# The end of a gated SSM/attention mix: one q half multiplied straight out of PSUM, the projection redistributed, the last tile added from PSUM and stored in halves

## The chip, the core and the metric

One core of one Trainium2 chip runs the whole kernel. The metric is the device time of one execution in microseconds (us); before the change it is 224.88 us, the median of three runs (224.69, 224.88 and 225.51). The profiled execution is another one, and its span, from its first to its last instruction, is 222.5 us.

The engines are named as in the profile: PE is TensorE (matmuls), PEld its weight loads, DVE is VectorE, ACT is ScalarE, POOL is GpSimd, SP is SyncE, which here only issues DMAs. "SPq" and "ACTq" are the sequencers of SP and ACT while they issue a DMA.

## The reference

The inputs are bf16 tensors of 2048 positions by 640 columns. Two branches read the same q, and a gate mixes them:

```
x = A_q;  g = sigmoid((x * gate_w).sum(-1, keepdims=True))
a = A_q * (long_convolution(shift(A_k) * A_v, A_ssm_k) + (shift(A_k) * A_v) * A_ssm_D)   # FFT of length 4096
b = local_attention(B_x @ wqkv; 32 heads of 20, window 8, dilation 2) @ wo
out = g * a + (1 - g) * b
```

The end of the kernel therefore needs three things for each output tile: `y`, the result of the last stage of the inverse transform; `g * q`, which is made earlier; and `(1 - g) * b`, the scaled output of the projection by `wo`. The output is `y * (g * q) + (1 - g) * b`.

## The kernel before, in words

The kernel is recorded by many small generators ("streams"): each yields a request for an engine, and a string (ORDER, L115 to L124) names, letter by letter, the stream whose request is granted next. So the order on every engine is written out by hand. The letter `s` grants a step of `outproj`, `t` a step of `final`, `u` and `v` a step of `load_q` for the first and the second half of q; a `-` takes the second engine that a request allows. Every engine works through its own list in order, and a wait of one instruction holds up all that stand behind it on that engine.

PSUM is cut into four slots of two banks (`plan = Steps(4)`). A matmul group takes a slot, or half of one, and the evacuation that reads the result gives it back.

The change lies in what happens after the last stage but one of the inverse transform (`inverse1`, L826 to L841, matmuls at L835, evacuated to `UC` by the helper at L243 on ACT and L245 on DVE). From there on four things are left:

- `final` (L893 to L930). The 16 output tiles of 128 positions are done in six groups of 3, 3, 2, 3, 3 and 2 tiles (`TAIL`). A group takes two PSUM slots: PE runs 32 small matmuls a tile (L912), and the result `y` lies in the first slot for columns 0 to 319 and in the second for columns 320 to 639. Both are copied to `yb`, one by ACT (L243) and one by DVE (L245), except the third group, where ACT copies both. Then DVE multiplies `yb` into the q tile in place (L924), adds the projection `bl` (L926), and SP stores the group with four DMAs (L929), one for each 32 partitions. In the last group ACT issues two of the four.
- `outproj` (L859 to L878). Each tile of the projection is done in two halves of 320 columns. A half is five matmuls (L869) into half a PSUM slot; ACT (L874), once DVE (L876), scales it by `omg`, which is 1 - g, and writes it to `bl`. Of the 32 halves 11 are done earlier in the kernel, 21 between and behind the groups of `final`: 4, 3, 4, 4, 4 and 2.
- `load_q` (L880 to L891). DVE multiplies the 16 tiles of q by g (L890). Eight of these stand between the steps of the first three groups.
- The end of the program (L965): SP waits for the landing of every DMA, and the engines meet at a barrier.

The DMAs that SP and ACT issue report their landing on eight semaphores (DMAHW0 to DMAHW7 in the instruction lists), which are given out in turn in the program's order. A DMA waits until the DMA that had its semaphore before it has landed.

Of the kernel before, what the change touches and what calls it, by code (L numbers as in the profile page):

```python
# [18 lines left out]
D = 640  # L19
# [29 lines left out]
KROWS = [(42, 64), (20, 42), (0, 20)]  # L49
TAIL = [(0, 3), (3, 3), (6, 2), (8, 3), (11, 3), (14, 2)]  # L50
# [65 lines left out]
a-aa-aw-wa-aw-ww-wiiai-iiaaiaa-aia-iii-aiaa-ii-iiii-ii-iiiicifffccccw-wwww-wwwwfwwwwf-wffffwwwwwwcwcccccwwwdw-wdwddddi-wfccccccii  # L116
-iiidfifddiiiieiifiiffiieidddiiiiiicddiwdxwexxxxxxxxxxccccffcfffffffffeccc-xcfcccccccccccccccccccccccccccccccccccccccccccidi-iiddd
ii-iddifd-iifxdddxedidffdfddefcicccii-iddiedd-icddlie-iiiyf-yddccdixiyyfy-xe-ydddexixdxddyyfyy-xcccxcccxffcccccccccccccciiiiciiccd
ciieddffdcccffdd-iiieiifiidididxdiffffffexididxdfeidid-i-xfxxyyy-yyexyey-xyyfyxccccccccciccccc-xcccc-idddidx-i-xxddddi-x-ijdddfjff
ejiddcciddcceiiiidddiiiiiffgg-ideieddd-ii-igigddiddeddjddeyjjyyyeeyyy-yyyy-yyyycc-yyyy-ycccccyyccccccccccccccclccccdddddz-zzd-zddd  # L120
z-zzzz-zzccczz-zzzzzz-zeddddedcdzdd-zedddoezdddd-zzo-zz-zjuddedddzedzz-zzzeezzz-zzooozz-z101-0010-1u111-111111-1o101-00o00-000000o
-00001011-1r-rr-r000u0r-r10111r00o00oooo2222-r0r-r000000000oqssss11110sssssss0s01111ssss2ss21111ssss222222222oooooooo222222244111p
313333p31333333333333413333uu4uuu444444444444444u54vv55u-5555-55-55-55-5555555tuut-ttssssssvvtvvstttstssssssv-tttvtttstssvv-ssvtvs
ttstst-ttssssssstttst-ttsssssssstttts-tssstt  # L124
# [91 lines left out]
def kernel(  # L216
# [642 lines left out]
    def outproj():  # L859
# [4 lines left out]
        for t in range(16):  # L864
            for n in range(2):
                g = yield Req("P", 0.0, [ev(f"oT{ft}") for ft in range(NDT)], take=1, half=1, pe=(5, 137.0, 272.0, 133.0))
                op = psum(g)[:, 0:320]
                for ft in range(NDT):
                    nc.tensor.matmul(op, lhsT=oT[:, ft].rearrange("p h m a -> p a (h m)")[:, t, :], rhs=wo[:, ft, 320 * n:320 * n + 320],  # L869
                                     start=(ft == 0), stop=(ft == NDT - 1), skip_group_check=True)  # L870
                r = yield Req("AD", dict(A=370.0, D=400.0), [g.done], give=g.banks)
# [5 lines left out]
            mark(f"bl{t}", r)  # L877
# [15 lines left out]
    def final():  # L893
        yield Req("N", 0.0, [ev("i10")])
        yb2 = p0.tile([128, 2, 3, D], BF, name="yb2", tag="H0")
        ybfree = [Ev(-1), Ev(-1)]
        for n, (t0, m) in enumerate(TAIL):
# [18 lines left out]
            es = []  # L916
            for k in range(2):
                r = yield Req("AD", n=320 * m, deps=[g.done, ybfree[n % 2]], give=[g.banks[k]])
# [51 lines left out]
```

## Time and profile before

| what | value |
|---|---|
| device time, median of 3 runs | 224.88 us |
| span of the profiled execution | 222.5 us |
| median less that span | 2.4 us |
| busy in the span: PE, DVE, ACT | 204.3, 185.0, 174.9 us |
| the last inverse-transform matmul (L835) to the first matmul of `final` | 1.1 us in which PE is idle |
| matmuls of `final` and the projection, 196.2 to 216.6 us | 20.4 us, PE busy for all of it |
| from the last matmul to the end of the span | 5.9 us |

The page's own time is the span; what lies around it, 2.4 us to the median, is the launch and the difference between the executions, and no view shows it in pieces. Times in the rows are us from the start of the span. In a timeline row the first number is the start, the second the time from the start of the first instruction of the row to the end of its last, "xN" the number of instructions merged in it, and a bracket at the end tells how long the engine was idle before and which work ended that. Instructions on one engine overlap by some tens of nanoseconds, so the start of the next row is the better measure of a step. In a row of groups the two numbers behind the bar are the busy time of all and the mean of one in ns.

### The profile page before, as it was taken

The numbers are of one execution on the slowest core, as the hardware profiler recorded it, in microseconds if no ns is written. First come the engines' busy times: TensorE is split into PE (matmuls) and PEld (weight loads), VectorE is DVE, ScalarE is ACT, GpSimd is POOL, SyncE is SP. The second block draws the span as 40 slices with busy tenths as digits, with TensorE's granted clock in tenths as the row PEclk, the third lists the DMA queues.
The fourth block names the chain that finished last, engine by engine and source line by source line (L and its number), as shares of the span: only waits on it lengthen the run. The fifth ranks groups of instructions, "written<-read, shape, count | busy, mean of one in ns | idle before, by whom it ended". The sixth has DMA issues, their size and how long they took to land.

```text
span 222.5 us, 8401 instructions
## 1 busy us (share of the span) xinstructions
PE 204.3 (92%) x3577; PEld 165.8 (75%) x3577; DVE 185.0 (83%) x261; ACT 174.9 (79%) x253; POOL 51.1 (23%) x129
## 2 busy tenths in 40 slices
PE   7999999999999999699997867999999999979990
PEld 3777987696777577466685756889888899979880
DVE  4745778997998898569898978998999997859992
ACT  0264487769998898599999988998999999478770
POOL 7980711470617044402450000000000000000000
PEclk9999999999999999999999699999999999999999
DMA  6999789599999999803993396678567082003645
GB/s 199 349 237 275 188 180 205 133 168 149 208 182 197 163 151 155 140 4 52 183 171 74 85 214 152 172 174 213 122 142 227 4 184 55 3 3 91 152 106 136
DMA packets 69049, 33.35 MB, mean 150 GB/s; under 512 B 51476, under 2 KB 66708, under 8 KB 69012
## 3 DMA queue, kind: packets, MB, share of 16 engines
q1 hardware_dynamic: 65684, 27.66, 61.3%
q0 software_dynamic: 2880, 4.90, 9.9%
q8 instruction: 28, 0.46, 1.0%
q10 hardware_dynamic: 448, 0.26, 0.4%
q14 instruction: 9, 0.07, 0.1%
HBM read 19.51 MB, written 2.62 MB: 100 GB/s over the span
## 4 chain that ended last, share of the span: by engine, by line
PE 51%; DVE 20%; ACT 10%; DMA 8%; issue 7%; POOL 2%; DVEq 0%; POOLq 0%; ACTq 0%
PE PS L568 14%; PE PS L521 8%; ACT ETall L650 6%; PE PS L835 6%; DMA kb<-stg 6%; DVE UC L245 5%; PE PS L869 4%; PE PS L724 4%; PE PS L674 3%; DVE SX L245 3%; PE PS L642 3%; DVE q L926 2%; DVE yb L245 2%; ACT H L243 2%; DVE q L924 2%
## 5 line engine op out<-in xcount | busy, mean ns | idle before, releaser
L650 ACT ACTIVATE ETall<-PS 121x912 bf16<-121x912 f32 (+1 forms) x80 | 63.8, 864 | 8.1 <-PE PS L642 7.7
L568 PE MATMUL PS<-xT,Wqk 128*128 128x342 bf16 (+1 forms) x300 | 49.7, 310 | 0.6 <-ACT stg L243 0.3
L243 ACT CAST UC<-PS 128x1024 bf16<-128x1024 f32 (+2 forms) x49 | 44.4, 1030 | 4.0 <-DVE UC L245 3.1
L568 PEld LDWEIGHTS <-Wqk 128*128 128x128 bf16 x300 | 27.4, 97 | 14.3 <-issue 0.5
L521 PE MATMUL PS<-WvT,xT 128*121 128x320 bf16 x180 | 27.5, 300 | 0.1
L467 DVE TENSOR_TENSOR KX<-KX 128x1280 bf16<-128x1280 bf16 x32 | 25.3, 820 | 0.3
L618 POOL DMA_DIRECT2D qb<-stg x29 | 14.6, 506 | 45.8 <-ACT stg L243 30.5
L869 PE MATMUL PS<-wo,oT 128*128 128x320 bf16 x160 | 24.4, 302 | 0.1
L521 PEld LDWEIGHTS <-xT 128*121 128x121 bf16 x180 | 23.4, 134 | 1.4
L243 ACT CAST stg<-PS 128x363 bf16<-128x363 f32 (+1 forms) x39 | 17.1, 471 | 7.8 <-PE PS L568 7.5
L869 PEld LDWEIGHTS <-oT 128*128 128x128 bf16 x160 | 21.1, 145 | 1.5 <-issue 0.5
L724 PEld LDWEIGHTS <-G 64*128 64x128 bf16 x512 | 18.2, 93 | 4.9 <-issue 3.7
L618 POOL DMA_DIRECT2D kb<-stg x36 | 18.1, 511 | 15.8 <-ACT stg L243 7.6
L642 PE MATMUL PS<-qb,kb 31*128 31x114 bf16 x576 | 16.0, 212 | 5.1 <-DMA kb<-stg 2.3
L245 DVE CAST stg<-PS 128x342 bf16<-128x342 f32 (+1 forms) x21 | 11.0, 522 | 11.7 <-PE PS L568 9.4
L642 PEld LDWEIGHTS <-kb 31*128 31x128 bf16 x576 | 9.4, 93 | 13.5 <-issue 9.8
L674 PEld LDWEIGHTS <-ETall 121*128 121x128 bf16 x576 | 17.4, 96 | 2.1 <-issue 0.5
L674 PE MATMUL PS<-VW,ETall 121*128 121x63 bf16 (+2 forms) x576 | 18.2, 184 | 0.6 <-DVE SX L245 0.3
L835 PE MATMUL PS<-F,Hw 128*128 128x128 bf16 x160 | 18.1, 219 | 0.0
L874 ACT ACTIVATE bl<-PS,omg 128x320 bf16<-128x320 f32 x31 | 16.1, 566 | 2.4 <-PE PS L869 1.9
L835 PEld LDWEIGHTS <-Hw 128*128 128x128 bf16 x160 | 17.9, 114 | 0.0
L245 DVE CAST UC<-PS 128x1024 bf16<-128x1024 f32 x13 | 15.3, 1219 | 2.6 <-ACT UC L243 1.2
(75 smaller groups left out, 334.1 us busy)
## 6 DMA issues: line engine op xcount, KB each, us to landing
xn<-in_A_q_dram SPq DMA_DIRECT2D x8, 320.0 KB
h_lin<-in_A_ssm_k_dram SPq DMA_DIRECT2D x16, 160.0 KB
vin<-in_A_v_dram SPq DMA_DIRECT2D x8, 320.0 KB
Hw<-H SPq DMA_DIRECT2D x8, 320.0 KB
q<-in_A_q_dram SPq DMA_DIRECT2D x8, 320.0 KB
Hw<-SX SPq DMA_DIRECT2D x8, 320.0 KB
kb<-stg POOLq DMA_DIRECT2D x28, 85.1 KB, 5.5
out_dram<-q SPq DMA_DIRECT2D x16, 120.0 KB
```

Of the source, the lines that this page charges most:

```text
L243: nc.scalar.copy(dst, src)
L245: nc.vector.tensor_copy(dst, src)
L467: eng.tensor_tensor(d, kin[:, n + 3 - j:n + 3 - j + m, :], w.to_broadcast([128, m, QC]), ALU.mult)
L521: nc.tensor.matmul(ps[0:BK, 0:320], lhsT=xT[:, dt, s0:s0 + BK], rhs=Wv[:, dt, 320 * hp:320 * hp + 320], start=(dt == 0), stop=(dt == NDT - 1))
L568: nc.tensor.matmul(ps[:, 0:n], lhsT=Wqk[:, dt, w, 128 * ft:128 * ft + 128], rhs=xT[:, dt, s0:s0 + n], start=(dt == 0), stop=(dt == NDT - 1))
L618: (nc.sync if near else nc.gpsimd).dma_start(dst[r0:r0 + rows, 0:wd], stg[fa - f0:fb - f0, 0:wd])
L642: nc.tensor.matmul(psum(g, h4 // 2)[:, h4 % 2, BQ * bb:BQ * bb + BQ], lhsT=kb[r:r + DH + NF, BK * b:BK * b + 128], rhs=qb[r:r + DH + NF, B ...
L650: nc.scalar.activation(ETall[0:BK, e, :, 0:BQ * nb], psum(g, k)[0:BK, :, 0:BQ * nb], ACT.Exp, scale=SCALE)
L674: nc.tensor.matmul(O[:, (b - b0) // 6, c0:c0 + 21 * nh], lhsT=ETall[0:BK, e, hh, BQ * bb:BQ * bb + 128], rhs=VW[0:BK, b, 4 * t + h4:4 * t ...
L724: nc.tensor.matmul(ps[:, c, 160 * jj:160 * jj + 160], lhsT=G[rows, j0 + jj, 64 - 64 * rr:192 - 64 * rr], rhs=Am[rows, rr].rearrange("p o ( ...
L835: nc.tensor.matmul(d, lhsT=st[(key, P)][:, c, o + il // 4, :, il % 4], rhs=M[:, k, :], start=(k == 0), stop=(k == 1), skip_group_check=True)
L869: nc.tensor.matmul(op, lhsT=oT[:, ft].rearrange("p h m a -> p a (h m)")[:, t, :], rhs=wo[:, ft, 320 * n:320 * n + 320], start=(ft == 0), s ...
```

## The change

`final` copies only the first half of the columns to `yb` (ACT, always). The second half is multiplied by q directly out of PSUM by DVE, and then the first half by a second, shorter multiply. The addition of `bl` and its store stay, but for the last tile (15) they fall away: there `outproj` waits until q * y of the tile is there (event `z15`), and one DVE instruction scales the projection half in PSUM by `omg` and adds the tile to it. Each half of that tile is then stored by two DMAs, one from SP and one from ACT, 64 partitions each. The two DMAs that ACT issued for the last group go to SP, and cover tile 14 alone.

The order changes too. The projection halves stand 2 ahead of the first group and 4, 3, 3, 3, 2 and 4 behind the six groups, and all eight multiplies of the second half of q stand ahead of the first group. Up to the last matmul of `inverse1` the order is the same as before.

```diff
+LATE = 15
...
             for n in range(2):
...
+                if t >= LATE:
+                    yield Req("D", 400.0, [g.done, ev(f"z{t}")], give=g.banks)
+                    reg = st["q1"][:, t % 8, 320 * n:320 * n + 320]
+                    nc.vector.scalar_tensor_tensor(reg, op, omg[:, t:t + 1], reg, ALU.mult, ALU.add)
+                    for gh in range(2):
+                        (nc.scalar if gh else nc.sync).dma_start(raw(outf, (32 * gh + 2 * t) * D + 320 * n, [[D, 2], [64 * D, 32], [1, 320]]), reg[64 * gh:64 * gh + 64])
+                    continue
...
-        yb2 = p0.tile([128, 2, 3, D], BF, name="yb2", tag="H0")
+        yb2 = p0.tile([128, 2, 3, 320], BF, name="yb2", tag="H0")
...
-            es = []
-            for k in range(2):
-                r = yield Req("AD", n=320 * m, deps=[g.done, ybfree[n % 2]], give=[g.banks[k]])
-                copy(r.eng, yb[:, 0:m, 320 * k:320 * k + 320].rearrange("p t (q c) -> p q t c", q=2),
-                     pss[k][:, :, 0:160 * m].rearrange("p q (t c) -> p q t c", c=160))
-                es.append(r.done)
-            yield Req("D", 68.0 + 0.52 * 640 * m, es + [ev(f"qg{t0 // 8}"), ev("qi1")])
             reg = st[f"q{t0 // 8}"][:, t0 % 8:t0 % 8 + m, :]
-            nc.vector.tensor_tensor(reg, yb[:, 0:m, :], reg, ALU.mult)
+            zs = [reg[:, :, 320 * k:320 * k + 320] for k in range(2)]
+            zq = [z.rearrange("p t (q c) -> p q t c", q=2) for z in zs]
+            y = [pss[k][:, :, 0:160 * m].rearrange("p q (t c) -> p q t c", c=160) for k in range(2)]
+            r0 = yield Req("A", n=320 * m, deps=[g.done, ybfree[n % 2]], give=[g.banks[0]])
+            nc.scalar.copy(yb[:, 0:m].rearrange("p t (q c) -> p q t c", q=2), y[0])
+            yield Req("D", 75.0 + 1.04 * 320 * m, [g.done, ev(f"qg{t0 // 8}"), ev("qi1")], give=[g.banks[1]])
+            nc.vector.tensor_tensor(zq[1], y[1], zq[1], ALU.mult)
+            r = yield Req("D", 68.0 + 0.52 * 320 * m, [r0.done])
+            nc.vector.tensor_tensor(zs[0], yb[:, 0:m], zs[0], ALU.mult)
...
+            m = min(m, LATE - t0)
+            reg = reg[:, 0:m]
...
             for gg in range(4):
-                (nc.scalar if n == len(TAIL) - 1 and gg > 1 else nc.sync).dma_start(raw(outf, (32 * (gg // 2) + gg % 2 + 2 * t0) * D, [[64 * D, 32], [2 * D, m], [1, D]]),
+                nc.sync.dma_start(raw(outf, (32 * (gg // 2) + gg % 2 + 2 * t0) * D, [[64 * D, 32], [2 * D, m], [1, D]]),
                                   reg[32 * gg:32 * gg + 32])
```

Three places show what moved. The first is ACT from its last evacuations of `inverse1` (`UC`) on; before, this is its list (`yb` is the copy of y, `bl` a projection half, `q_3452` the second half of q):

```order
L243 CAST UC<-PS 128x128x8 x14
L243 CAST yb_3616<-PS 128x2x3x160
L874 ACTIVATE bl<-PS,omg 128x320 x4
L243 CAST yb_3616<-PS 128x2x3x160
L874 ACTIVATE bl<-PS,omg 128x320 x3
L243 CAST yb_3616<-PS 128x2x2x160 x2
L874 ACTIVATE bl<-PS,omg 128x320 x3
L243 CAST yb_3616<-PS 128x2x3x160
L874 ACTIVATE bl<-PS,omg 128x320 x4
L243 CAST yb_3616<-PS 128x2x3x160
L874 ACTIVATE bl<-PS,omg 128x320 x4
L243 CAST yb_3616<-PS 128x2x2x160
```

And this is ACT's list at the same place with the change:

```order
L244 CAST UC<-PS 128x128x8 x14
L882 ACTIVATE bl<-PS,omg 128x320 x2
L930 CAST yb_3616<-PS 128x2x3x160
L882 ACTIVATE bl<-PS,omg 128x320 x4
L930 CAST yb_3616<-PS 128x2x3x160
L882 ACTIVATE bl<-PS,omg 128x320 x3
L930 CAST yb_3616<-PS 128x2x2x160
L882 ACTIVATE bl<-PS,omg 128x320 x3
L930 CAST yb_3616<-PS 128x2x3x160
L882 ACTIVATE bl<-PS,omg 128x320 x3
L930 CAST yb_3616<-PS 128x2x3x160
L882 ACTIVATE bl<-PS,omg 128x320 x2
```

Two projection halves now stand ahead of the first copy, and the fifth group has two behind it instead of four; the matmuls stand in the same order on PE.

The second place is DVE in the last two groups. Before:

```order
L245 CAST yb_3616<-PS 128x2x3x160
L924 TENSOR_TENSOR q_3452<-yb_3616,q_3452 128x1920
L926 TENSOR_TENSOR q_3452<-q_3452,bl 128x1920
L245 CAST yb_3616<-PS 128x2x2x160
L924 TENSOR_TENSOR q_3452<-yb_3616,q_3452 128x1280
L926 TENSOR_TENSOR q_3452<-q_3452,bl 128x1280
```

With the change:

```order
L932 TENSOR_TENSOR q_3452<-PS,q_3452 128x2x3x160
L934 TENSOR_TENSOR q_3452<-yb_3616,q_3452 128x3x320
L941 TENSOR_TENSOR q_3452<-q_3452,bl 128x1920
L932 TENSOR_TENSOR q_3452<-PS,q_3452 128x2x2x160
L934 TENSOR_TENSOR q_3452<-yb_3616,q_3452 128x2x320
L941 TENSOR_TENSOR q_3452<-q_3452,bl 128x640
L875 SCALAR_TENSOR_TENSOR q_3452<-PS,omg,q_3452 128x320 x2
```

The copy from PSUM has become the multiply, the other multiply is half as wide, and two instructions for tile 15 end the list.

The third place is SP's list of stores from the fifth group on, with the semaphores that each waits for. Before:

```order
L929 DMA out_dram<-q_3452 32x3x640 [waits DMAHW5_49,DVE_49]
L929 DMA out_dram<-q_3452 32x3x640 [waits DMAHW6_49]
L929 DMA out_dram<-q_3452 32x3x640 [waits DMAHW7_49]
L929 DMA out_dram<-q_3452 32x3x640 [waits DMAHW1_49]
L929 DMA out_dram<-q_3452 32x2x640 [waits DMAHW3_49,DVE_49]
L929 DMA out_dram<-q_3452 32x2x640 [waits DMAHW4_49]
```

With the change:

```order
L943 DMA out_dram<-q_3452 32x3x640 [waits DMAHW5_49,DVE_49]
L943 DMA out_dram<-q_3452 32x3x640 [waits DMAHW6_49]
L943 DMA out_dram<-q_3452 32x3x640 [waits DMAHW7_49]
L943 DMA out_dram<-q_3452 32x3x640 [waits DMAHW2_49]
L943 DMA out_dram<-q_3452 32x640 [waits DMAHW3_49,DVE_49]
L943 DMA out_dram<-q_3452 32x640 [waits DMAHW4_49]
L943 DMA out_dram<-q_3452 32x640 [waits DMAHW5_49]
L943 DMA out_dram<-q_3452 32x640 [waits DMAHW6_49]
L877 DMA out_dram<-q_3452 2x32x320 [waits DMAHW7_49,DVE_49]
L877 DMA out_dram<-q_3452 2x32x320 [waits DMAHW0_49,DVE_49]
```

SP issues six stores after the fifth group instead of two. The one that had DMAHW0 before SP's last store is ACT's first store of tile 15, and those that had DMAHW5, 6 and 7 are stores of the fifth group. ACT's two stores, of tile 15, each wait for DVE and for stores of the third and fourth group.

More of the change, by code (lines that the diff above doesn't have):

```diff
@@ L115 @@
 ORDER = """
[L116 to L124, printed above, removed]
+a-aa-aw-wa-aw-ww-wiiai-iiaaiaa-aia-iii-aiaa-ii-iiii-ii-iiiicifffccccw-wwww-wwwwfwwwwf-wffffwwwwwwcwcccccwwwdw-wdwddddi-wfcccccci
+i-iiidfifddiiiieiifiiffiieidddiiiiiicddiwdxwexxxxxxxxxxccccffcfffffffffeccc-xcfcccccccccccccccccccccccccccccccccccccccccccidi-ii
+dddii-iddifd-iifxdddxedidffdfddefcicccii-iddiedd-icddlie-iiiyf-yddccdixiyyfy-xe-ydddexixdxddyyfyy-xcccxcccxffcccccccccccccciiiic
+iiccdciieddffdcccffdd-iiieiifiidididxdiffffffexididxdfeidid-i-xfxxyyy-yyexyey-xyyfyxccccccccciccccc-xcccc-idddidx-i-xxddddi-x-ij
+dddfjffejiddcciddcceiiiidddiiiiiffgg-ideieddd-ii-igigddiddeddjddeyjjyyyeeyyy-yyyy-yyyycc-yyyy-ycccccyyccccccccccccccclccccdddddz
+-zzd-zdddz-zzzz-zzccczz-zzzzzz-zeddddedcdzdd-zedddoezdddd-zzo-zz-zjuddedddzedzz-zzzeezzz-zzooozz-z101-0010-1u111-111111-1o101-00
+o00-000000o-00001011-1r-rr-r000u0r-r10111r00o00oooo2222-r0r-r000000000oqssss11110sssssss0s01111ssss2ss21111ssss222222222oooooooo
+222222244111p313333p31333333333333413333uu4uuu444444444444444u54vv55u-5555-55-55-55-5555555ssssuuvvvvvvvvvvttttttsssssssstttttts
+sssssttttttssssssttttttsssssstttttssssttttttsssstssss
 """
@@ L876, in outproj @@
                     nc.vector.tensor_scalar(dst, op, omg[:, t:t + 1], None, ALU.mult)
-            mark(f"bl{t}", r)
+            if t < LATE:
+                mark(f"bl{t}", r)
         mark("outproj", g)
@@ L915, in final @@
             yb = yb2[:, n % 2]
-            es = []
-            for k in range(2):
-                r = yield Req("AD", n=320 * m, deps=[g.done, ybfree[n % 2]], give=[g.banks[k]])
-                copy(r.eng, yb[:, 0:m, 320 * k:320 * k + 320].rearrange("p t (q c) -> p q t c", q=2),
-                     pss[k][:, :, 0:160 * m].rearrange("p q (t c) -> p q t c", c=160))
-                es.append(r.done)
-            yield Req("D", 68.0 + 0.52 * 640 * m, es + [ev(f"qg{t0 // 8}"), ev("qi1")])
-            reg = st[f"q{t0 // 8}"][:, t0 % 8:t0 % 8 + m, :]
-            nc.vector.tensor_tensor(reg, yb[:, 0:m, :], reg, ALU.mult)
+            reg = st[f"q{t0 // 8}"][:, t0 % 8:t0 % 8 + m, :]
+            zs = [reg[:, :, 320 * k:320 * k + 320] for k in range(2)]
[7 more added lines that the diff above has]
+            nc.vector.tensor_tensor(zs[0], yb[:, 0:m], zs[0], ALU.mult)
+            ybfree[n % 2] = r.done
+            for t in range(t0, t0 + m):
+                mark(f"z{t}", r)
+            m = min(m, LATE - t0)
+            reg = reg[:, 0:m]
             r = yield Req("D", 100.0 + 0.52 * 640 * m, [ev(f"bl{t}") for t in range(t0, t0 + m)])
             nc.vector.tensor_tensor(reg, reg, st["bl"][:, t0:t0 + m, :], ALU.add)
-            ybfree[n % 2] = r.done
             for gg in range(4):
-                (nc.scalar if n == len(TAIL) - 1 and gg > 1 else nc.sync).dma_start(raw(outf, (32 * (gg // 2) + gg % 2 + 2 * t0) * D, [[64 * D, 32], [2 * D, m], [1, D]]),
+                nc.sync.dma_start(raw(outf, (32 * (gg // 2) + gg % 2 + 2 * t0) * D, [[64 * D, 32], [2 * D, m], [1, D]]),
                                   reg[32 * gg:32 * gg + 32])
```

## The prediction, written before the changed kernel was run

> **What bounds the kernel now.** I read the page first, then the busy time by stretches of the end, the chain of waits, and the timelines of PE, ACT, DVE and SP.
>
> ```profile
> span 222.5 us, 8401 instructions
> ```
>
> The busy time by stretches (columns: stretch, length, busy time and instruction count of each engine, granted clock, share of the DMA engines, GB/s):
>
> ```profile
> 195.10:196.20 1.10, 0.00 (x0) 0.00 (x0) 0.00 (x0) 1.07 (x2) 0.00 (x0) 1.00 0.00 0
> 196.20:216.60 20.40, 20.38 (x617) 18.26 (x616) 18.64 (x25) 15.35 (x26) 0.00 (x0) 1.00 0.37 93
> 216.60:218.30 1.70, 0.06 (x1) 0.00 (x0) 1.58 (x2) 0.53 (x1) 0.00 (x0) 1.00 0.69 169
> 218.30:220.40 2.10, 0.00 (x0) 0.00 (x0) 0.00 (x0) 0.00 (x0) 0.00 (x0) 1.00 0.92 248
> 220.40:222.50 2.10, 0.00 (x0) 0.00 (x0) 0.00 (x0) 0.00 (x0) 0.00 (x0) 0.85 0.01 4
> ```
>
> Four parts, then: 1.1 us in which PE is idle while ACT ends its evacuations; 20.4 us of PE without a gap; 1.7 us of ACT and DVE behind the last matmul; and 4.2 us without any compute, in the first half of which the stores drain. The chain of waits goes through DVE in the long part:
>
> ```profile
> 195.14 1.04 ACT UC L243
> 196.22 1.06 PE PS L912 x96
> ...
> 215.69 0.74 DVE yb L245
> ...
> 216.53 0.84 DVE q L924
> ...
> 217.46 0.83 DVE q L926
> ```
>
> PE and DVE are both nearly full there (20.38 and 18.64 of 20.40), so a saving on one alone would be held by the other. The change touches both, and the end of the stores as well, so I follow all three.
>
> **PE.** Its timeline:
>
> ```profile
> 196.22 1.02 PE L912 MATMUL PS<-UC,SX 32*32 32x160 bf16 x96 [1.14 <-ACT UC L243]
> 197.17 2.94 PE L869 MATMUL PS<-wo,oT 128*128 128x320 bf16 x20
> 200.04 1.03 PE L912 MATMUL PS<-UC,SX 32*32 32x160 bf16 x96
> 200.99 2.26 PE L869 MATMUL PS<-wo,oT 128*128 128x320 bf16 x15
> 203.18 0.76 PE L912 MATMUL PS<-UC,SX 32*32 32x160 bf16 x64
> 203.87 2.94 PE L869 MATMUL PS<-wo,oT 128*128 128x320 bf16 x20
> ...
> 215.08 1.58 PE L869 MATMUL PS<-wo,oT 128*128 128x320 bf16 x10
> ```
>
> By the starts, a group of three tiles takes 0.95 us (196.22 to 197.17), one of two 0.69, four projection halves 2.87 (197.17 to 200.04), three 2.19, so a further half 0.68 and two halves 1.51. Before, PE ends at 215.08 + 1.51 = 216.59.
>
> No matmul is added or removed; two halves move into the gap from 195.08 (196.22 - 1.14) on. They need only PSUM and the projection's inputs, and the slots that they take are those whose reading ends with this row of DVE and with the first of these three on ACT, both by 194.5:
>
> ```profile
> 189.82 4.62 DVE L245 CAST UC<-PS 128x1024 bf16<-128x1024 f32 x4 [0.58 <-PE PS L835]
> 193.32 2.84 ACT L243 CAST UC<-PS 128x1024 bf16<-128x1024 f32 x3 [3.07 <-DVE UC L245]
> ```
>
> They take till 196.59, 0.37 us past the old start of the first group, which itself waits for ACT's last evacuation (till 196.16). The same work then follows in the order 3 tiles, 4 halves, 3, 3 halves, 2, 3 halves, 3, 3 halves, 3, 2 halves, 2, 4 halves: 195.08 + 1.51 + 4 x 0.95 + 2 x 0.69 + 2 x 2.87 + 3 x 2.19 + 1.51 = 215.59. **PE ends 1.0 us earlier.** If the gap were not filled, this term would be nothing.
>
> **DVE.** The prices, from the groups of instructions:
>
> ```profile
> L686 DVE TENSOR_TENSOR VW<-PS,rd 114x960 bf16<-114x960 f32 x8 | 9.3, 1158 | 0.3
> L686 DVE TENSOR_TENSOR VW<-PS,rd 114x480 bf16<-114x480 f32 x8 | 5.3, 658 | 0.4
> L756 DVE TENSOR_TENSOR SX<-UC,SX 128x960 bf16<-128x960 bf16 x10 | 6.5, 651 | 0.0
> L756 DVE TENSOR_TENSOR SX<-UC,SX 128x640 bf16<-128x640 bf16 x1 | 0.5, 489 | 0.0
> L245 DVE CAST yb<-PS 128x960 bf16<-128x960 f32 x4 | 4.6, 1153 | 2.2 <-PE PS L912 2.2
> L245 DVE CAST yb<-PS 128x640 bf16<-128x640 f32 x1 | 0.8, 818 | 0.0
> L924 DVE TENSOR_TENSOR q<-yb,q 128x1920 bf16<-128x1920 bf16 x4 | 4.6, 1159 | 0.4
> L876 DVE TENSOR_SCALAR bl<-PS,omg 128x320 bf16<-128x320 f32 x1 | 0.5, 546 | 0.0
> ```
>
> The kernel already has a two-input DVE instruction that reads PSUM (L686), at 1158 ns for 960 elements: the multiply costs what the copy did (1153). The other multiply shrinks from 1159 to 651. So a group of three saves 0.5 us of DVE. The eight multiplies by g (one takes 0.38 us, two 0.67, so 0.30 for each further one) leave the stretch for the idle time ahead of it, where they run from 195.0 to 197.5 behind the two that end there now, done as the first group's matmuls are (196.59 + 0.95 = 197.54).
>
> ```profile
> 194.35 0.67 DVE L890 TENSOR_SCALAR q<-q,g_nat 128x640 bf16<-128x640 bf16 x2
> 201.26 0.38 DVE L890 TENSOR_SCALAR q<-q,g_nat 128x640 bf16<-128x640 bf16 x1
> ```
>
> Together that is about 5 us less in the stretch (8 x 0.30 and 6 x 0.5 at most). DVE stops being the bound and waits for PE; this saving is worth nothing by itself. It is only the cover for the first term: with DVE as full as before, PE's 1.0 us would have been lost to it.
>
> The exact point is the fifth group. Its second half behind it is done on PE at 195.08 + 16.95 = 212.03 (the sum above up to there). ACT needs 0.64 from there, as from 216.59 to the end of the last row here:
>
> ```profile
> 216.70 0.53 ACT L874 ACTIVATE bl<-PS,omg 128x320 bf16<-128x320 f32 x1 [0.15 <-PE PS L869]
> ```
>
> so DVE adds the group from 212.7 to 213.9 (1.16, as L926 before), where before it ended at 215.69. Behind that stand on DVE: the multiply of the last group out of PSUM 0.82 (price of the 640-element copy), the other 0.49, the addition of tile 14 0.49, and two scale-and-add instructions for tile 15. No row has those; the nearest is the scaling of the same shape at 0.546, and the bounds are 0.49 (the 640-element multiply in SBUF) and 0.66 (480 elements from PSUM). I take 0.55. With the 0.08 us by which neighbours without a wait overlap, four times, tile 14 is done at 215.6, the first half of tile 15 at 216.1 and the second at 216.5: 1.8 us ahead of the 218.29 (217.46 + 0.83) of before. Were the multiply out of PSUM as dear as copy and multiply together (1.15 + 0.65, my upper end), the fifth group would hold PE and DVE for 0.5 us more; at the lower end, the row of L686, nothing.
>
> **The stores.** This is where I expect the gain to shrink. SP's timeline, and the last issues on SP and ACT:
>
> ```profile
> 201.37 2.67 SPq L929 DMA_DIRECT2D out_dram<-q  x4
> 208.60 1.74 SPq L929 DMA_DIRECT2D out_dram<-q  x4
> 212.13 1.75 SPq L929 DMA_DIRECT2D out_dram<-q  x4
> 215.72 1.33 SPq L929 DMA_DIRECT2D out_dram<-q  x2
> 217.10 2.01 SPq L929 DMA_DIRECT2D out_dram<-q  x4
> 218.68 0.43 SPq L929 DMA_DIRECT2D out_dram<-q  x1
> 218.81 0.39 ACTq L929 DMA_DIRECT2D out_dram<-q  x1
> ```
>
> An issue takes 0.43 us, and the next starts 0.05 later; size does not matter (the groups of 3 and of 2 tiles take 1.75 and 1.74). The end follows the last issue (218.81) by 222.46 - 218.81 = 3.65 us: landing, the waits for it, the barrier. SP's waits say how long a landing is:
>
> ```profile
> SPq L965 <- DMA out_dram<-q: 1.5, 2, 1.1
> ```
>
> SP, done issuing at 219.1, waits 1.1 us for ACT's store of 218.32, which lands at some 220.3: 2.0 us after its issue.
>
> Now the changed queue. The fifth group is ready at 213.9 and its four issues last till 215.7. By then tile 14 is ready (215.6), so its four follow without a pause, and then the two of tile 15: the tenth issue starts at 215.7 + 5 x 0.48 = 218.1. SP's last store also waits until ACT's first store of tile 15 has landed, 216.1 + 2.0 = 218.1, since it takes over that one's semaphore: both come at the same time. Last issue 218.1 + 3.65 = 221.8. **The compute ends 1.8 us earlier, the program 0.7 us,** because ten issues in a row on SP are 4.6 us long. Against 222.46 that is a gain of 0.66 us. I take the 2.4 us around the span as unchanged: 224.88 - 0.66 = 224.2 us.
>
> The wait on ACT's store costs nothing while SP is this late, and if SP were quick it would hold the last store until 218.1 all the same. Behind it stands only the end of the program.
>
> **A rule that speaks otherwise.** The row that carries this is 1.75 us for four issues. The Trainium skill, page DMA: Bandwidth & Descriptors, section Issuing engines are not separate DMA queues, holds that starting DMAs from several engines saves only the sequencer's time, which is usually small relative to the DMA itself. In this trace an issue takes 0.43 us and a landing 2.0, so one is small, but ten are not. By that rule the end would follow the compute, which is the first rival below.
>
> **The rivals.**
>
> *The full gain.* The stores keep up and the end follows the last DVE instruction as before (218.29 to 222.46, 4.17): 216.5 + 4.17 = 220.7, so 223.1 us. For it: the DMA engines are less loaded, since by 218.1 only tiles 14 and 15 are under way, against a share of 0.92 from 218.30 on before. Against it: the ten issues and the wait on ACT's landing, either of which alone gives 218.1. A quicker landing of 0.3 us, counted twice, would give 223.6. Chance of this side 0.22.
>
> *The issue stalls.* Four issues took 2.67 instead of 1.75 us at 201.37, and two 1.33 instead of 0.8 at 215.72. Before, the second stall was hidden behind DVE; in the changed queue there is no slack from 213.9 on, so one stall of 0.5 to 0.9 goes straight to the end: 224.7 to 225.1 us, no gain. For it: 2 of the 6 groups had one. Chance 0.22.
>
> *Slower: a landing holds the queue.* SP's last four issues wait for landings of stores 2.0 to 2.9 us older (three of the fifth group's, and ACT's first). It decides once a landing takes longer than that; to be slower than before by 0.5% the last issue would have to start 1.8 us later than I put it, so ACT's store would have to take 3.8 us instead of 2.0. Rows of other DMAs do show that much:
>
> ```profile
> kb<-stg POOLq DMA_DIRECT2D x28, 85.1 KB, 5.5
> ```
>
> With 5.5 us (these are moves within the chip's memory, issued by POOL, amid many) the last issue would start at 221.6, the time would be 227.7 us. Against it: the store that I can see took 2.0 with the DMA engines at 0.92. Chance 0.07.
>
> **How the numbers follow.** My own case, 224.2 us, has 0.49, and a range of its own from 223.8 to 224.6 (0.2 on each price of landing and issue). About 0.5%, 1.1 us, is what a measurement here can tell from no change, so faster means below 223.8 and slower above 226.0. My own case and the stall fall within; the full gain makes most of faster, with some of my case's lower edge: 0.25. Slower is the third rival: 0.07. The rest, 0.68, is no change. The range reaches to the full gain on the one side and past the stall on the other: 223.2 to 225.2 us, leaving out about 0.1 on each side. The bound of 0.5 us on the PSUM multiply lies within it.
>
> **What would show it.** Right: in the new timeline ten matmuls of the projection ahead of the first group and PE idle for less than 0.3 us there; the multiply out of PSUM at 1.1 to 1.2 us for 960 elements; DVE with gaps before each group; ten issues on SP with no pause from about 214 to 218.5; the last DVE instruction 1.5 us or more ahead of 218.3, and the span under 0.9 us shorter. The end then follows the compute by about 5.3 us instead of 4.2. Wrong: SP waiting between its last stores for anything but ACT's landing, the last DVE instruction no earlier than 217.5, or a span below 221.2, which would say that the issues on SP do not set the end.

## The result, and the profile after

The change is slower. Its median is 227.25 us over 20 runs (224.91 to 229.48), against 224.74 us for the kernel before, over 20 runs too (222.52 to 227.54): a ratio of 1.0121, 95% interval 1.0094 to 1.0148, a loss of 2.1 to 3.3 us. The ratio, here and below, leaves out the slow executions, those over 1.5% above the fastest of the same kernel, so it is not the quotient of the two medians. The forecast was 224.2 us and its range ended at 225.2.

The span of the profiled execution grew only from 222.5 to 223.1 us:

```profile
span 223.1 us, 8403 instructions
```

That understates the loss, because executions of one program differ ahead of the changed part. The code is the same up to the last matmul of the inverse transform, and yet it starts at 194.85 us in the profiled execution before and at 193.71 in the one after. These rows of PE's timeline, one of before and then those of after, show it (the row of the first group has 94 of its 96 matmuls, since the view ends there):

```profile
194.85 0.22 PE L835 MATMUL PS<-F,Hw 128*128 128x128 bf16 x1
```

```profile
193.71 0.22 PE L836 MATMUL PS<-F,Hw 128*128 128x128 bf16 x1
193.76 1.53 PE L870 MATMUL PS<-wo,oT 128*128 128x320 bf16 x10
195.22 1.01 PE L921 MATMUL PS<-UC,SX 32*32 32x160 bf16 x94
...
211.37 2.94 PE L870 MATMUL PS<-wo,oT 128*128 128x320 bf16 x20
```

So from here on I count from the start of that matmul, and call the rest of the span the tail. Before, the tail is 222.46 - 194.85 = 27.6 us; after, 223.11 - 193.71 = 29.4. A second profiled execution of the change gave 29.6. The traces show a loss of 1.8 to 2.0 us.

The compute did what was forecast. The two projection halves stand right behind the inverse transform, and the idle 1.1 us of PE is gone: the first group starts 1.51 us into the tail (195.22). In the groups of instructions of after, the multiply out of PSUM costs 1158 ns for 960 elements (L932), the other 648 (L934), and the scale-and-add of a half tile 544 (L875):

```profile
L932 DVE TENSOR_TENSOR q<-PS,q 128x960 bf16<-128x960 f32 x4 | 4.6, 1158 | 2.3 <-PE PS L921 2.2
L934 DVE TENSOR_TENSOR q<-yb,q 128x960 bf16<-128x960 bf16 x4 | 2.6, 648 | 0.0
L875 DVE SCALAR_TENSOR_TENSOR q<-PS,omg,q 128x320 bf16<-128x320 f32 x2 | 1.0, 544 | 0.0
```

DVE's timeline ends with these rows, which answer to L924 and L926 at 216.53 and 217.46 before:

```profile
211.35 1.16 DVE L941 TENSOR_TENSOR q<-q,bl 128x1920 bf16<-128x1920 bf16 x1 [0.25 <-ACT bl L882]
212.43 0.81 DVE L932 TENSOR_TENSOR q<-PS,q 128x640 bf16<-128x640 f32 x1
213.16 0.48 DVE L934 TENSOR_TENSOR q<-yb,q 128x640 bf16<-128x640 bf16 x1
213.74 0.49 DVE L941 TENSOR_TENSOR q<-q,bl 128x640 bf16<-128x640 bf16 x1
214.15 1.00 DVE L875 SCALAR_TENSOR_TENSOR q<-PS,omg,q 128x320 bf16<-128x320 f32 x2
```

The last DVE instruction ends at 215.15, 21.4 us into the tail; before, 218.29, 23.4. **The compute ends 2.0 us earlier, and the program 1.8 us later.** All of the loss lies behind the compute: the end follows the last DVE instruction by 8.0 us, where before it was 4.2. The busy time by stretches shows what fills them (columns: stretch, length, busy time of PE, PEld, DVE, ACT and POOL, granted clock, share of the 16 DMA engines, GB/s):

```profile
215.20:217.70 2.50, 0.00 (x0) 0.00 (x0) 0.00 (x0) 0.00 (x0) 0.00 (x0) 1.00 0.58 146
217.70:219.90 2.20, 0.00 (x0) 0.00 (x0) 0.00 (x0) 0.00 (x0) 0.00 (x0) 0.60 0.13 38
219.90:221.90 2.00, 0.00 (x0) 0.00 (x0) 0.00 (x0) 0.00 (x0) 0.00 (x0) 0.50 0.06 19
```

Before, the stretch without compute had a DMA share of 0.92 and 248 GB/s, and then was empty. Now from 217.7 on all that is left to store is part of tile 15, some 120 KB by these rows (2.2 x 38 + 2.0 x 19), and it moves at 38 GB/s with a share of 0.13. Two of 16 engines busy all the time would be 0.125. SP and ACT issue like this:

```profile
212.53 4.09 SPq L943 DMA_DIRECT2D out_dram<-q  x8
216.72 1.48 SPq L877 DMA_DIRECT2D out_dram<-q  x2
```

```profile
214.73 1.78 ACTq L877 DMA_DIRECT2D out_dram<-q  x2
```

And SP's waits say how long the last landing takes:

```profile
SPq L979 <- DMA out_dram<-q: 3.1, 1, 3.1
...
SPq L877 <- DMA out_dram<-q: 0.3, 1, 0.3
```

SP is done issuing at 218.2 (216.72 + 1.48) and then waits some 3.1 us, till 221.4, where before it waited 1.1 us. The last store lands 3.7 us after its issue started, not 2.0. The wait on ACT's first store, the one that I had reckoned with, is 0.3 us.

This suggested the theory for the experiments: **the stores of tile 15 run on two DMA engines only.** Their destination is `[[D, 2], [64 * D, 32], [1, 320]]`, with a slowest dimension of 2 (a pattern is a list of pairs of step and count, the slowest first); all other stores have one of 32. The rivals were the short pieces (640 bytes instead of 1280), the ten issues in a row on SP, and the wait of SP for ACT's landing.

### The profile page after: what moved, and what is told of

The parts are those of the page before. It is cut to its first block, busy times and chain, and to the rows that moved or that the text cites. A ratio compares the mean times of both kernels' runs of the same rounds, so it can differ in the third digit from the quotient of the medians.

```text
span 223.1 us, 8403 instructions
## 1 busy us (share of the span) xinstructions
PE 204.0 (91%) x3577; PEld 165.4 (74%) x3577; DVE 183.3 (82%) x263; ACT 173.7 (78%) x251; POOL 51.0 (23%) x129
## 4 chain that ended last, share of the span: by engine, by line
PE 59%; DVE 11%; DMA 10%; ACT 9%; issue 5%; POOL 1%; DVEq 0%; SPq 0%; POOLq 0%; ACTq 0%
PE PS L569 15%; PE PS L870 9%; PE PS L522 8%; PE PS L836 8%; ACT ETall L651 5%; DMA kb<-stg 5%; PE PS L725 4%; PE PS L675 3%; DVE UC L246 3%; PE PS L643 3%; DMA xn<-in_A_q_dram 3%; DMA qb<-stg 3%; DVE SX L246 2%; ACT H L244 2%; PE PS L921 2%
## 5 line engine op out<-in xcount | busy, mean ns | idle before, releaser
L522 PEld LDWEIGHTS <-xT 128*121 128x121 bf16 x180 | 23.4, 134 | 1.4
L246 DVE CAST SX<-PS 128x1024 bf16<-128x1024 f32 (+2 forms) x13 | 14.6, 1160 | 2.9 <-PE PS L725 1.7
```

The source lines that it names most:

```text
L246: nc.vector.tensor_copy(dst, src)
L522: nc.tensor.matmul(ps[0:BK, 0:320], lhsT=xT[:, dt, s0:s0 + BK], rhs=Wv[:, dt, 320 * hp:320 * hp + 320], start=(dt == 0), stop=(dt == NDT - 1))
```

## The experiments

All times in this table are us from the start of the last inverse-transform matmul, from one profiled execution each; the ratio is that of timed runs to the kernel before, with its 95% interval. Where a kernel was run twice, both stand; of the order alone the second trace is read.

| kernel | last DVE end | last store issued | last store landed | end of the tail | ratio |
|---|---|---|---|---|---|
| before | 23.44 | 23.95 | 25.92 | 27.60 | 1 |
| the change | 21.45 | 23.95 | 27.69 | 29.40 | 1.0121 (1.0094 to 1.0148) |
| the change, second time | 21.48 | 24.74 | 27.89 | 29.60 | 1.0112 (1.0060 to 1.0164) |
| tile 15 by 32 partitions, whole rows | 21.45 | 23.31 | 24.82 | 26.54 | 0.9989 (0.9951 to 1.0027) |
| tile 15 by 32 partitions, halves | 21.50 | 25.15 | 26.65 | 27.76 | 1.0016 (0.9973 to 1.0060) |
| before, with the new store pattern | 23.44 | 24.94 | 33.02 | 34.67 | 1.0259 (1.0191 to 1.0327) |
| order and multiply, tile 15 as before | 22.03 | 22.54 | 24.52 | 26.18 | 0.9969 (0.9923 to 1.0016) |
| the same, second time | 22.03 | 22.55 | 24.53 | 26.18 | 0.9953 (0.9911 to 0.9994) |
| tile 15 by 32 partitions, tile 14 on two queues | 21.78 | 23.42 | 25.12 | 26.86 | 0.9949 (0.9914 to 0.9983) |
| order alone | | | | | 0.9944 (0.9893 to 0.9995) |
| order alone, second time | 22.79 | 23.31 | 25.34 | 26.99 | 0.9953 (0.9911 to 0.9996) |
| multiply out of PSUM alone | 23.23 | 23.75 | 25.79 | 27.45 | 1.0015 (0.9975 to 1.0055) |
| tiles 14 and 15 stored together | 21.86 | 22.37 | 24.67 | 26.35 | 0.9958 (0.9903 to 1.0013) |
| the same, second time | 21.60 | 22.12 | 24.17 | 25.85 | 0.9973 (0.9932 to 1.0014) |

### Only the store pattern of tile 15 changed

The change as it is, but tile 15 is stored whole behind its second half, by four DMAs of 32 partitions, two from SP and two from ACT:

```diff
-                    for gh in range(2):
-                        (nc.scalar if gh else nc.sync).dma_start(raw(outf, (32 * gh + 2 * t) * D + 320 * n, [[D, 2], [64 * D, 32], [1, 320]]), reg[64 * gh:64 * gh + 64])
+                    for gg in range(4 * n):
+                        (nc.scalar if gg > 1 else nc.sync).dma_start(raw(outf, (32 * (gg // 2) + gg % 2 + 2 * t) * D, [[64 * D, 32], [1, D]]), st["q1"][32 * gg:32 * gg + 32, t % 8])
```

> The changed kernel with one edit: tile 15 is stored after both its halves by four DMAs of 32 partitions by 640 columns (two from SP, two from ACT), instead of two DMAs of 64 partitions by 320 columns a half. Bytes, and the issues on SP and on ACT, stay as they are (10 from the fifth group on, and 2). Theory N (narrow stores): in the profile of the changed kernel the DMA engines are busy at a share of 0.13 from 217.7 to 219.9 us and 0.06 after it, about 2 of 16, while tile 15 drains, and SP waits 3.1 us for a landing; the pattern of these stores, with a slowest dimension of 2 in the output, puts each on two engines. With a slowest dimension of 32 the last landing takes 2.0 us after its issue as before, so the loss of 2.5 us goes and what is left of the forecast's gain shows: 223.9 to 224.7 us, ratio 0.997 to 1.000. Theory U (the loss comes from ahead of the end, or from the ten issues on SP): the ratio stays near 1.01. The Trainium skill, page DMA: Bandwidth & Descriptors, section Why a DMA increments its semaphore by 16 and not by 1, states that the largest number up to 16 that divides the slowest dimension of both sides is the number of engines used, which would be 2 and then 16.

The ratio fell from 1.0121 to 0.9989 and the tail from 29.4 to 26.5 us. The compute is the same: the last DVE instruction ends at 21.45 in both. SP still has ten issues in a row and starts the last one 0.6 us earlier, but now it lands 1.5 us after its issue. SP's timeline (the first of its nine issues is still the fourth group's), its wait at the end, and the stretches:

```profile
211.73 5.91 SPq L943 DMA_DIRECT2D out_dram<-q  x9
217.74 0.83 SPq L877 DMA_DIRECT2D out_dram<-q  x2
```

```profile
SPq L979 <- DMA out_dram<-q: 1.1, 1, 1.1
```

```profile
216.40:218.60 2.20, 0.00 (x0) 0.00 (x0) 0.00 (x0) 0.00 (x0) 0.00 (x0) 1.00 0.62 166
218.60:219.80 1.20, 0.00 (x0) 0.00 (x0) 0.00 (x0) 0.00 (x0) 0.00 (x0) 0.54 0.26 68
```

The wait behind the last issue is 1.1 us again, as before the change, and the share no longer sits at 0.13. What made the change slower is in the pattern of these four stores, and not in SP's ten issues, which are still there.

### Halves, but by 32 partitions

This one keeps the stores in two halves of 640-byte pieces and changes the partitions alone, so each half takes four DMAs instead of two:

```diff
-                    for gh in range(2):
-                        (nc.scalar if gh else nc.sync).dma_start(raw(outf, (32 * gh + 2 * t) * D + 320 * n, [[D, 2], [64 * D, 32], [1, 320]]), reg[64 * gh:64 * gh + 64])
+                    for gg in range(4):
+                        (nc.scalar if gg > 1 else nc.sync).dma_start(raw(outf, (32 * (gg // 2) + gg % 2 + 2 * t) * D + 320 * n, [[64 * D, 32], [1, 320]]), reg[32 * gg:32 * gg + 32])
```

> The changed kernel with tile 15 still stored half by half, in pieces of 640 bytes, but each half by four DMAs of 32 partitions (two from SP, two from ACT). SP issues 12 stores from the fifth group on instead of 10, ACT 4 instead of 2. Theory N (two engines for each store is the cost): the last landing takes 2.0 us again; two more issues of 0.48 us on SP cost about 1.0 us against the run with four DMAs, so 224.8 to 225.5 us, ratio 1.000 to 1.004. Theory P (the pieces of 640 bytes instead of 1280 are the cost): no better than the change, ratio near 1.012.

Measured: 1.0016, tail 27.8. The short pieces are not the cause: the last store lands 1.5 us after its issue (25.15 to 26.65), as with whole rows. The last issue starts 1.8 us later than with whole rows (25.15 against 23.31). Some 0.6 of that is one issue in the fifth group, which took 1.25 us where it took 0.65 there; the rest goes to twelve issues in a row on SP instead of ten, two of which wait for older landings:

```profile
SPq L943 <- DMA out_dram<-q: 0.7, 2, 0.5
```

The end is only 1.2 us later, because it follows the last landing by 1.1 us here (27.76 - 26.65) and by 1.7 with whole rows (26.54 - 24.82). Why that differs is not known.

### The pattern alone, in the kernel before

The kernel before with its own order and compute; only the last four DMAs, those of the last group, take the form of the change, one for each tile and 64 partitions:

```diff
+                if n < len(TAIL) - 1:
...
+                else:
+                    gh, tt = gg // 2, gg % 2
+                    (nc.scalar if gh else nc.sync).dma_start(raw(outf, (32 * gh + 2 * (t0 + tt)) * D, [[D, 2], [64 * D, 32], [1, D]]),
+                                                             reg[64 * gh:64 * gh + 64, tt])
```

> The kernel before with the suspected cost alone: its last group of two tiles is stored by four DMAs of 64 partitions by 640 columns, one for each tile and half of the partitions, whose output pattern has a slowest dimension of 2, instead of four DMAs of 32 partitions. The number of issues, the engines that issue them, the bytes and the pieces of 1280 bytes stay. Theory N: these stores run on two DMA engines, the end after the last DVE instruction grows from 4.2 us to 5.5 to 7.5, the time to 226 to 228 us. Theories U and P: as before, within 0.3%.

Measured: 1.0259, and the tail grew by 7.1 us (27.6 to 34.7). The end comes 11.2 us after the last DVE instruction (34.67 - 23.44), where 5.5 to 7.5 had been expected. Number of DMAs, bytes (80 KB each), queues and compute are those of before. SP's waits, and three of the stretches:

```profile
SPq L970 <- DMA out_dram<-q: 8.2, 2, 5.7
```

```profile
219.70:222.00 2.30, 0.00 (x0) 0.00 (x0) 0.00 (x0) 0.00 (x0) 0.00 (x0) 0.50 0.12 33
222.00:224.00 2.00, 0.00 (x0) 0.00 (x0) 0.00 (x0) 0.00 (x0) 0.00 (x0) 0.50 0.13 49
224.00:226.00 2.00, 0.00 (x0) 0.00 (x0) 0.00 (x0) 0.00 (x0) 0.00 (x0) 0.50 0.13 50
```

For over 6 us the share stands at 0.12 to 0.13 with stores outstanding all the while, at up to 50 GB/s; before, the last stores moved at 248. Four stores in flight from two queues do not get beyond two engines' worth: 4 x 82 KB at 50 GB/s are 6.6 us. That is what the expectation had missed. Counted packet by packet in this trace, two are under way for 1.8 of the 2.0 us from 224.0 on and never more than three; in the kernel before, from 218.30 to 220.40, it is mostly 13 to 18.

One more thing changes with the pattern: these DMAs are of 64 partitions each, and all stores with a slowest dimension of 32 are of 32 partitions. The number of partitions alone does not make a DMA slow. In the kernel before SP also issues the copies `Hw<-SX` (L820), of 64 partitions each and not to DRAM, with a slowest dimension of 64, and while they alone move data, the share is 0.90:

```profile
158.50:159.50 1.00, 1.00 (x22) 0.91 (x22) 1.00 (x3) 1.00 (x3) 0.00 (x0) 1.00 0.90 184
```

A store of 64 partitions with a longer slowest dimension was not run.

The row that a rule has to answer to is the share of 0.13. The Trainium skill, page DMA: Bandwidth & Descriptors, section Why a DMA increments its semaphore by 16 and not by 1, gives a rule for it: a DMA takes the largest number of engines up to 16 that divides the slowest dimension longer than one on both of its sides, and for DMAs issued by SP and ACT always the lowest-numbered ones. A slowest dimension of 2 gives two engines, a share of 0.125, and always the same two. The trace agrees, with 0.12 to 0.13 for four stores together; no view here names the engines.

### Order and multiply, without the last tile's path

The change, but tile 15 goes through `bl` like all others (LATE = 16), the order is that of the change with the last addition behind all halves, and the last group's four stores are those of before, two on SP and two on ACT:

```diff
-LATE = 15
+LATE = 16
...
-sssssttttttssssssttttttsssssstttttssssttttttsssstssss
+sssssttttttssssssttttttsssssstttttssssttttttsssssssst
...
-                nc.sync.dma_start(raw(outf, (32 * (gg // 2) + gg % 2 + 2 * t0) * D, [[64 * D, 32], [2 * D, m], [1, D]]),
+                (nc.scalar if n == len(TAIL) - 1 and gg > 1 else nc.sync).dma_start(raw(outf, (32 * (gg // 2) + gg % 2 + 2 * t0) * D, [[64 * D, 32], [2 * D, m], [1, D]]),
```

> The change without its last part: tile 15 is projected, scaled to SBUF, added and stored with tile 14 as before the change; q half out of PSUM and the projection halves ahead of the groups stay, and the last addition stands behind all halves. Theory N: PE ends 1.0 us earlier than before, then 0.64 us of ACT, 0.83 us of DVE and 4.2 us of stores: 1.0 to 1.3 us gained, 223.4 to 223.8 us, ratio 0.994 to 0.996. Theory U (something ahead of the end got slower by the change of order): no gain or a loss, ratio 1.00 to 1.01.

And its second time, on another chip:

> The change without its last part once more (tile 15 like the others, its projection half scaled to SBUF), beside the run with the joint store: the last DVE instruction at 22.0 us after the last inverse matmul, the end at 26.2; 0.5 us slower than the joint store, ratio 0.992 to 0.996.

Measured: 0.9969 and 0.9953, tail 26.18 in both traces, 1.4 us less than before. The last DVE instruction ends 0.6 us later than in the change (22.03), because it waits for the scaled projection (the row is of the second trace):

```profile
217.01 0.83 DVE L941 TENSOR_TENSOR q<-q,bl 128x1280 bf16<-128x1280 bf16 x1 [1.27 <-ACT bl L882]
```

But the end follows it by 4.15 us, as before (4.17), since the queues are empty by then. It beats the kernel with tile 15's new path and good stores by 0.36 us in the traces, although that one's compute ends 0.6 us sooner. The reading that fits is the price of ten issues in a row on SP; the timed ratios do not tell the two kernels apart.

### Order alone, multiply alone

The first has the code of before and only the new order of the change (halves 2 ahead and 4, 3, 3, 3, 2, 4 behind, all multiplies by g ahead); its diff is the string ORDER. The second has the group code of the kernel above (LATE = 16, multiply out of PSUM) in the order of before.

> The kernel before with the new order alone: two projection halves ahead of the first group, 4, 3, 3, 3, 2 and 4 behind the groups, all eight multiplies by g ahead of the first group; y is copied to SBUF by both engines and multiplied there, and the stores are as before. DVE's work from the first group on is then 4 x 3.5 + 1.8 + 2.7 = 18.5 us, PE's 20.5. Theory O (the order is the gain): PE sets the end, the last DVE instruction comes 1.0 to 1.3 us earlier, the end 26.2 to 26.6 us after the last inverse matmul (27.6 before), ratio 0.994 to 0.998. Theory M (only the cheaper multiply makes room on DVE): DVE keeps the end where it was, 27.3 or more, ratio 0.998 to 1.002.

> The new order alone in the kernel before, once more, for a trace of an undisturbed execution and more times. Theory O (the order is nearly the whole gain): the last DVE instruction 22.0 to 22.4 us after the last inverse matmul (23.4 before, 22.0 with order and multiply together), the end 26.2 to 26.6. If order and multiply need each other: DVE at 22.7 or later, the end at 26.9 or later. Ratio 0.993 to 0.998.

> The multiply out of PSUM alone: the changed code of the groups with the order of before on every engine, tile 15 treated like the others, stores as before (the copies of the third group are one on ACT, and the other half is multiplied by DVE). DVE is relieved by 0.5 us a group, PE starts the first group where it did. Theory O: PE still ends 21.5 us after the last inverse matmul and the end is 27.3 to 27.6 us after it, ratio 0.998 to 1.001. Theory M: 26.5 or less, ratio 0.994 to 0.996.

Order alone: 0.9944 and 0.9953; the tail of the second one's trace is 26.99, 0.6 us less than before. Multiply alone: 1.0015, tail 27.45, 0.15 us less. Together, in the kernel above, 1.42: in the traces the two are worth 0.66 us more than their sum. Order alone came out as the second expectation has it for the case that the two need each other: DVE at 22.79, the end at 26.99. The reason is in PE's timelines. With the order alone, PE fills the gap but waits for DVE's copy further on, and its last matmul ends 0.8 us later than with both (21.4 instead of 20.6 us into the tail); with the multiply alone the gap stays:

```profile
215.65 0.84 PE L869 MATMUL PS<-wo,oT 128*128 128x320 bf16 x5 [0.34 <-DVE yb L245]
```

```profile
195.37 1.02 PE L921 MATMUL PS<-UC,SX 32*32 32x160 bf16 x96 [1.15 <-ACT UC L244]
```

So the lighter DVE is cover for the order, worth almost nothing by itself, as the prediction had it. The timed runs agree on the multiply (its interval holds 1), but they do not show that order and multiply together are better than the order alone: the intervals of the two lie on each other.

### The change again, and three ways to store the last tiles

The change unchanged, on the chip of the next kernel:

> The changed kernel as it is, once more on this chip, for a second trace. Theory N: the last two stores land 3 to 4 us after their issue again, the DMA engines at a share of about 0.13 for some 2 us ahead of that, and the end 29 to 30.5 us after the last inverse-transform matmul; 226.5 to 228 us.

Measured: 1.0112, tail 29.60, with 2.5 us of waiting for the last landing. The loss repeats.

The next has the whole-row stores of tile 15 and gives two of tile 14's four stores to ACT, so that SP has eight in a row instead of ten:

```diff
-                nc.sync.dma_start(raw(outf, (32 * (gg // 2) + gg % 2 + 2 * t0) * D, [[64 * D, 32], [2 * D, m], [1, D]]),
+                (nc.scalar if n == len(TAIL) - 1 and gg > 1 else nc.sync).dma_start(raw(outf, (32 * (gg // 2) + gg % 2 + 2 * t0) * D, [[64 * D, 32], [2 * D, m], [1, D]]),
```

> The version that should beat both: the change with tile 15 stored by four DMAs of 32 partitions by 640 columns, and tile 14's four stores shared as before the change, two from SP and two from ACT. SP issues 8 stores from the fifth group on instead of 10, ACT 4. From the start of the last inverse-transform matmul to the end of the span it is 27.6 us before, 29.4 with the change and 26.5 with the wide stores alone. Theory N with the queue on SP as the next bound: the last issue moves from 23.3 to some 22.3 us after that matmul and the end to 25.5 or 25.9; 222.7 to 223.5 us, ratio 0.991 to 0.995. If SP's queue were not the bound: 26.5 again.

Measured: 0.9949 (0.9914 to 0.9983), the only interval of all that ends clearly below 1. Its trace does not show why: the tail, 26.86, is longer than with ten issues on SP (26.54), and than the 25.5 to 25.9 that were expected. Two things went wrong in that execution. PE stood still in the middle of the fifth group, and SP's queue stalled: six issues took 3.97 us where 6 x 0.48 are 2.9, nearly all of it in the second one, which took 1.59.

```profile
212.70 0.32 PE L921 MATMUL PS<-UC,SX 32*32 32x160 bf16 x22 [0.39 <-issue]
```

```profile
213.59 3.97 SPq L943 DMA_DIRECT2D out_dram<-q  x6
```

The last stores the two tiles together behind tile 15's second half, by four DMAs in all:

```diff
-                    for gh in range(2):
-                        (nc.scalar if gh else nc.sync).dma_start(raw(outf, (32 * gh + 2 * t) * D + 320 * n, [[D, 2], [64 * D, 32], [1, 320]]), reg[64 * gh:64 * gh + 64])
+                    for gg in range(4 * n):
+                        (nc.scalar if gg > 1 else nc.sync).dma_start(raw(outf, (32 * (gg // 2) + gg % 2 + 2 * t - 2) * D, [[64 * D, 32], [2 * D, 2], [1, D]]),
+                                                                     st["q1"][32 * gg:32 * gg + 32, t % 8 - 1:t % 8 + 1])
...
-            for gg in range(4):
+            for gg in range(4 if n < len(TAIL) - 1 else 0):
```

> The change with its stores alone undone: tile 15 is still added straight from PSUM, but tiles 14 and 15 are stored together behind it by four DMAs of 32 partitions by two tiles, two from SP and two from ACT, as in the kernel before. SP issues 6 stores from the fifth group on instead of 10, and has slack for the stall that its second store of that group shows. Theory N with the queue on SP as the second cost: the last DVE instruction comes 21.5 us after the last inverse matmul as in the change, the last issue 0.5 us behind it, and the end 4.2 us behind it, at 25.6 (27.6 before, 29.4 and 29.6 in the two traces of the change, 26.5 with wide stores and ten issues): 222.6 to 223.4 us, ratio 0.989 to 0.994. If the ten issues were not a cost of their own: 26.5 again.

> The joint store of tiles 14 and 15 behind the addition from PSUM, once more, for a trace and more times: the last DVE instruction 21.5 us after the last inverse matmul unless PE waits for its own instructions in the fifth group as in the first trace, the end 25.6 to 26.4; ratio 0.991 to 0.998.

Measured: 0.9958 and 0.9973, tails 26.35 and 25.85. The second is the shortest tail of all, 1.75 us less than before, with the end 4.25 us behind the last DVE instruction. In the first, PE had a gap of 0.5 us in the fifth group, as above, and the tail misses the 25.6 that was expected. The lead of 0.5 us over the kernel with tile 15 as before, expected above, is 0.3 in the second trace and none in the first. The timed runs give it no lead either.

What the timed runs allow to say of a better version: order alone, order with multiply, and the kernel with tile 14 on two queues each have an interval that ends below 1, at best by a hair (0.9995, 0.9996, 0.9994 and 0.9983). All lie at 0.994 to 0.997 and can't be told apart. The last of these beats both kernels most clearly: its median is 223.51 us, where that of before was 225.2 and that of the change 227.25 on that chip. With the lowest of so many intervals ending at 0.9983, and a trace that is no shorter, this is not proof of a better kernel.

## Why the prediction was wrong

**The step that failed** is the one behind the compute: "Last issue 218.1 + 3.65 = 221.8". The 3.65 holds a landing of 2.0 us, "2.0 us after its issue", read from a store of 32 partitions, and it was put on stores of another pattern. Measured from the last inverse-transform matmul, the forecast end is 221.8 - 194.85 = 26.95 us; it was 29.40. Of the 2.45 us between them 1.8 lie behind the last issue (223.11 - 217.66 = 5.45 instead of 3.65): this store took 3.7 us to land, at the rate of two engines. The other 0.7 is the last issue, at 23.95 instead of 23.25. I had given SP 4.2 us from the first to the tenth issue and it took 5.1: 0.3 is the wait for ACT's store, 0.5 a stall of one issue in the fifth group, 0.1 the ninth issue, which took 0.59 instead of 0.43. Against that the fifth group was ready 0.2 us earlier than forecast.

The second trace of the change divides otherwise. Of its 2.65 us 1.2 lie behind the last issue (29.60 - 24.74 = 4.86) and 1.5 ahead of it; of these 0.95 is the stalled issue of the fifth group, which took 1.38 us, and 0.3 again the wait for ACT's store. So the landing is the largest term in both, but not the whole miss. The price of the pattern with all that hangs on it is the difference to the kernel that changes it alone: 29.40 and 29.60 against 26.54.

With the store pattern alone put right, the tail is 26.54 where 26.95 was forecast, and the timed ratio 0.9989 where 224.2 / 224.88 = 0.9970 lies well within its interval, as does 1. The last issue is then at 23.31, forecast 23.25, and what is left of the difference is a landing of 1.5 us instead of 2.0, of stores half as large (40 KB). So the rest of the sum stood but for the stalls, and the landing put on these stores is the term that was mis-sized.

Point by point:

- **PE ends 1.0 us earlier.** Right. The first group starts 1.51 us into the tail, forecast 1.74 (196.59 - 194.85). PE ends at 211.37 + 2.87 = 214.24, 20.5 us into the tail; forecast 20.7.
- **The prices of the DVE instructions.** Right: 1158, 648 and 544 ns, where 1158, 651 and 550 had been taken from other lines of the trace.
- **"It is only the cover for the first term."** Right in the traces: 0.6 us for the order alone, 0.15 for the multiply alone, 1.4 for both.
- **The compute ends 1.8 us earlier.** Right: 2.0.
- **Ten issues in a row on SP are a cost.** Right in kind: with good stores the end follows the compute by 5.1 us where SP has ten issues (26.54 - 21.45; 5.3 was forecast), and by 4.2 to 4.5 in the kernels with tile 15 as before and with the joint store, where it has six. The tails are 26.5 against 25.9 to 26.4, though the compute of those ends up to 0.6 us later. The kernel with eight issues, at 26.86, does not fit in; its one trace has the two delays named above. This was the place where I set the Trainium skill (page DMA: Bandwidth & Descriptors, section Issuing engines are not separate DMA queues) against the row of 1.75 us for four issues. The traces bear the row out, with a few tenths of a us of the tail; the timed runs cannot show it.
- **The wait on ACT's store "costs nothing while SP is this late".** Nearly: 0.3 us in both traces of the change.
- **The issue stalls** (chance 0.22) were the rule: in all 14 traces one issue of the fifth group's burst takes longer than 0.43 us, by 0.2 to 1.2. The rival was underpriced, and only because the landing cost more was it the smaller part: 0.5 and 0.95 us in the change's two traces.
- **"Slower: a landing holds the queue"** (chance 0.07) was the nearest rival, and it was underpriced on the wrong ground: "the store that I can see took 2.0 with the DMA engines at 0.92". That row is of a store with a slowest dimension of 32 and says nothing of one with 2. It also asked only whether a late landing would hold SP's queue. The larger part came from what stands behind it: the program ends with the last landing, so a longer landing is paid even if no issue waits.

What the diff showed and I did not price: the destination of the new stores, `[[D, 2], [64 * D, 32], [1, 320]]` beside `[[64 * D, 32], [2 * D, m], [1, D]]`. Fewer DMAs of more partitions looked like a saving of issues; it was a cut of the rate from 248 GB/s to about 50 at most.

**What stays open.** The timed loss, 2.1 to 3.3 us, is somewhat more than the 1.8 and 2.0 of the two traces; the first trace is of the quickest of the change's 20 runs. Why executions reach the last inverse-transform matmul at times from 193.7 to 196.6 us was not looked into (the code is the same up to there in all these kernels). Neither was the cause of PE's gap in the fifth group: 0.1 to 0.5 us in six of the 14 traces, 0.1 of it in the change's second one and none in its first. The stalls of single issues are open too. In each of the 14 traces a packet of 16 KB of the queue that the page calls instruction starts within 0.8 us ahead of the stalled issue of the fifth group; that the one causes the other is not shown.

## What to carry to other kernels

Price a new store by its pattern, not by its bytes: read the share of the DMA engines while nothing else is under way, and look at the slowest dimension of the pattern, since here 2 instead of 32 cost 7.1 us of one trace for four stores of 80 KB. Where the program ends with a store, its landing stands on the path in full, so splitting the last tile only pays if the pieces land as fast as the whole did and are not queued behind a row of other issues. When spans of single executions differ ahead of the change, compare the traces from the last common instruction on.

## What the runs showed that was not expected

- A store with a slowest dimension of 2 occupies 0.12 to 0.13 of the DMA engines' time and moves up to 50 GB/s, and several of them in flight, from both queues, do not add up.
- Such a store is also dearer to issue. Two of them took ACT 1.78 us (the row at 214.73), where the two by 32 partitions of the kernel before take 0.87. With the same 80 KB each but the new pattern they take 2.00. The rows are of ACT's timeline, of the kernel before and of the kernel before with the new pattern:

```profile
218.32 0.87 ACTq L929 DMA_DIRECT2D out_dram<-q  x2
```

```profile
217.80 2.00 ACTq L934 DMA_DIRECT2D out_dram<-q  x2
```

- In every trace one issue of SP in the fifth group's burst, nearly always the second, takes 0.6 to 1.6 us instead of 0.43, whatever the last stores look like.
